# Seven half-size products in place of eight: Strassen's algorithm in the second MLP product

## The chip, the core and the metric

The kernel runs on one core of one Trainium2 chip. The metric is the device time of one execution in microseconds (us), the median over runs. The engines named below are TensorE (PE; its weight loads are PEld), VectorE (DVE), ScalarE (ACT), GpSimd (POOL) and SyncE (SP, which here issues loads, transposes and some stores). Each runs its own instructions in program order; they meet at semaphores.

## The reference, cut to what matters

```python
# attention: q, k, v are (8, 8, 576, 64); phi gives 128 features per position
q_p = phi(q, cos_w, sin_w); k_p = phi(k, cos_w, sin_w)      # relu(x)*cos, relu(x)*sin
kv = einsum('bhsf,bhsd->bhfd', k_p, v); z = sum(k_p, axis=2)
attn = einsum('bhsf,bhfd->bhsd', q_p, kv) / (einsum('bhsf,bhf->bhs', q_p, z) + 1e-06)
x = attn.transpose(0, 2, 1, 3).reshape(8, 576, 512)
# mixer: U (576, 32), V (32, 576), w_ch1 (512, 2048), w_ch2 (2048, 512)
u = x + (x.transpose(0, 2, 1) @ U @ V).transpose(0, 2, 1)
out = u + maximum(u @ w_ch1, 0) @ w_ch2
```

Inputs and output are fp32. The first MLP product is `u @ w_ch1`, the second is `hid @ w_ch2` with `hid` the relu of the first. The kernel multiplies in bf16 and sums in fp32.

## The kernel before

A batch has 576 rows: four chunks of 128 and a tail of 64. Two batches make a pair, and their two tails make one more chunk of 128 rows.

The attention of a batch goes through `q_prep` and `k_prep` (relu times cos or sin, ten instructions of 128x512 each for q and for k, on DVE or ACT), `v_prep` (casts of v to bf16, mostly on POOL), transposes of q by DMA (`qtr_dma`), `kv_unit`, `x_unit` (matmuls into the PSUM tile `x_ps`, which has one buffer, then reciprocal and scaling on DVE), `A_unit` (x times U), and `u_unit` (V times that into `va_ps`, then DVE adds x and writes `u_bf`). `utr_dma` transposes `u_bf` into `uT`.

The MLP of a batch: `g1_main(b, j)` makes 128 of the 2048 hidden columns for four chunks of rows, with four matmuls of 512 columns into `g_ps`; ACT takes the relu into `hid`. `g1_tail` does the same for a pair's tail chunk with matmuls of 128 columns, into `hid_tl`. `g2_part(pr, cc, part)` does a quarter of the second product for one chunk of rows: four matmuls of 512 columns, of the 16 that sum into a bank of `o_ps`. After the fourth quarter DVE adds `u_bf` and writes `o_sb`, which is stored.

The order is written by hand. `slots` is a list of such units: for each pair, 16 of `g1_main` for the even batch, 16 for the odd, four of `g1_tail`, 36 of `g2_part` (in the first pair the even batch's second product stands behind its first). One slot is four matmuls of 512 columns. `todo` names what is issued behind each slot: the attention of later batches, by `PLAN` and `attention_plan`. A `PLAN` entry has the slot of `kv_unit`, the place of the preparations against it, the engines for q and k, the place of the q transposes, and the places of the next batch's loads. `spare(at)` picks the PSUM tag for a unit issued behind slot `at`. PSUM has the tags `g` (three banks), `o` (two), `X` (two banks as one tile) and `T` (one).

## Time and profile before

| | us |
|---|---|
| median of three runs (lowest, highest) | 312.73 (312.23, 314.8) |
| span of the profiled execution, first to last instruction | 314.4 |
| PE busy | 305.0 |
| DVE busy | 154.3 |
| ACT busy | 136.3 |
| POOL busy | 53.0 |
| first product, `g1_main` matmuls busy (512) | 117.6 |
| second product, `g2_part` matmuls on `hid` and `hid_tl` busy (592) | 134.8 |

The profile gives no other time of its execution than the span; it lies at the upper end of the three runs. Busy times of PE contain the overlap of one matmul with the next, so a rate is read from the start of one to the start of the next. In the groups of the profile a line holds: code line, engine, operation, tiles written and read, shapes, count, busy time, mean ns of one, and the idle time ahead with what ended it. In a timeline a line holds start, length (of several merged: from the first start to the last end), engine, code line, operation, tiles.

### The profile page before, as it was taken

The numbers are of one execution on the slowest core, as the hardware profiler recorded it, in microseconds if no ns is written. First come the engines' busy times: TensorE is split into PE (matmuls) and PEld (weight loads), VectorE is DVE, ScalarE is ACT, GpSimd is POOL, SyncE is SP. The second block draws the span as 40 slices with busy tenths as digits, with TensorE's granted clock in tenths as the row PEclk, the third lists the DMA queues.
The fourth block names the chain that finished last, engine by engine and source line by source line (L and its number), as shares of the span: only waits on it lengthen the run. The fifth ranks groups of instructions, "written<-read, shape, count | busy, mean of one in ns | idle before, by whom it ended". The sixth has DMA issues, their size and how long they took to land.

```text
span 314.4 us, 5674 instructions
## 1 busy us (share of the span) xinstructions
PE 305.0 (97%) x2305; PEld 159.2 (51%) x2305; DVE 154.3 (49%) x341; ACT 136.3 (43%) x229; POOL 53.0 (17%) x96
## 2 busy tenths in 40 slices
PE   5989999999999899999999999999999999999995
PEld 2665555445745344474455444574455444474443
DVE  4787845696778567036525585036526530002111
ACT  2835660265560256659500266659500266640000
POOL 8410400240041106102321310002321100000000
PEclk9789999999999999999999999999999999999999
DMA  7999799969997979993699769942791140001131
GB/s 211 353 248 253 175 186 263 292 154 238 300 131 170 250 197 206 217 294 108 158 204 318 242 101 170 301 118 52 167 167 69 67 86 0 0 2 67 67 100 69
DMA packets 86027, 53.21 MB, mean 169 GB/s; under 512 B 54258, under 2 KB 83218, under 8 KB 86002
## 3 DMA queue, kind: packets, MB, share of 16 engines
q1 hardware_dynamic: 79298, 41.36, 56.9%
q0 software_dynamic: 6560, 11.43, 14.5%
q8 instruction: 18, 0.29, 0.4%
q14 instruction: 7, 0.06, 0.1%
q10 hardware_dynamic: 144, 0.07, 0.1%
HBM read 36.86 MB, written 9.44 MB: 147 GB/s over the span
## 4 chain that ended last, share of the span: by engine, by line
PE 84%; DMA 7%; DVE 5%; ACT 2%; issue 1%; DVEq 0%; ACTq 0%
PE o_ps L587 36%; PE g_ps L534 32%; PE gt_ps L554 5%; PE kv_ps L294 3%; DMA vst<-in_v_dram 3%; PE x_ps L401 2%; DMA q_tlT<-q_tl 2%; PE va_ps L446 2%; DMA uT<-u_bf 2%; DVE q_p L260 2%; DVE k_p L260 1%; ACT k_p L258 1%; PE t_ps L311 1%; PE a_ps L426 1%; ACT v_ext L108 1%
## 5 line engine op out<-in xcount | busy, mean ns | idle before, releaser
L543 ACT ACTIVATE hid<-g_ps 128x512 bf16<-128x512 f32 x128 | 76.3, 598 | 106.2 <-PE g_ps L534 106.1
L587 PE MATMUL o_ps<-w_bf,hid 128*128 128x512 bf16 (+2 forms) x528 | 120.0, 372 | 0.0
L534 PE MATMUL g_ps<-uT,w_bf 128*128 128x512 bf16 x512 | 117.6, 379 | 1.0 <-DMA uT<-u_bf 1.0
L534 PEld LDWEIGHTS <-w_bf 128*128 128x128 bf16 x512 | 48.9, 98 | 59.2 <-issue 2.0
L587 PEld LDWEIGHTS <-hid 128*128 128x128 bf16 x528 | 48.3, 98 | 50.7 <-issue 0.8
L597 DVE TENSOR_TENSOR o_sb<-u_bf,o_ps 128x512 f32<-128x512 bf16 (+2 forms) x33 | 22.1, 669 | 56.3 <-PE o_ps L587 56.2
L608 POOL DMA_DIRECT2D out_dram<-o_sb x24 | 15.2, 633 | 128.3 <-DVE o_sb L597 67.2
L453 DVE TENSOR_TENSOR u_bf<-x_bf,va_ps 128x512 bf16<-128x512 bf16 x32 | 21.8, 685 | 10.0 <-PE va_ps L446 9.9
L110 POOL CAST v_ext<-vst 128x512 bf16<-128x512 f32 (+1 forms) x28 | 20.0, 739 | 38.1 <-DMA vst<-in_v_dram 35.6
L110 DVE CAST kv<-kv_ps 128x260 bf16<-128x260 f32 x15 | 6.4, 429 | 38.0 <-PE kv_ps L294 38.0
L411 DVE TENSOR_TENSOR x_bf<-x_ps,rec 128x512 bf16<-128x512 f32 x28 | 19.4, 691 | 1.0
L358 DVE TENSOR_SCALAR rec<-x_ps 128x8 f32<-128x8 f32 (+1 forms) x35 | 5.8, 165 | 23.9 <-PE x_ps L401 23.4
L554 PE MATMUL gt_ps<-uT_tl,w_bf 128*128 128x128 bf16 x256 | 15.9, 219 | 0.0
L554 PEld LDWEIGHTS <-w_bf 128*128 128x128 bf16 x256 | 14.7, 98 | 0.9
L260 DVE TENSOR_SCALAR q_p<-qst,cosw 128x512 bf16<-128x512 f32 x24 | 13.7, 581 | 3.0 <-DMA qst<-in_q_dram 3.0
L587 PE MATMUL o_ps<-w_bf,hid_tl 128*128 128x512 bf16 x64 | 14.8, 379 | 0.0
L401 PEld LDWEIGHTS <-q_pT 128*128 128x128 bf16 x224 | 10.7, 98 | 6.6 <-DVE x_bf L411 0.6
L294 PEld LDWEIGHTS <-k_p 128*128 128x128 bf16 x256 | 11.2, 97 | 4.3 <-ACT v_tl L108 1.1
L258 ACT ACTIVATE k_p<-kst,sinw 128x512 bf16<-128x512 f32 x19 | 13.3, 712 | 0.0
L294 PE MATMUL kv_ps<-v_ext,k_p 128*128 128x65 bf16 x256 | 11.8, 193 | 1.0 <-ACT v_tl L108 0.8
L561 ACT ACTIVATE hid_tl<-gt_ps 128x512 bf16<-128x512 f32 x16 | 9.6, 598 | 6.6 <-PE gt_ps L554 6.6
L446 PE MATMUL va_ps<-A_sb,V_bf 128*128 128x512 bf16 x32 | 12.1, 379 | 0.1
(125 smaller groups left out, 235.5 us busy)
## 6 DMA issues: line engine op xcount, KB each, us to landing
qst<-in_q_dram SPq DMA_DIRECT2D x14, 512.0 KB, 6.1
kst<-in_k_dram SPq DMA_DIRECT2D x14, 512.0 KB, 8.5
vst<-in_v_dram SPq DMA_DIRECT2D x12, 512.0 KB, 8.4
out_dram<-o_sb POOLq DMA_DIRECT2D x24, 256.0 KB, 3.1
w_bf<-in_moe_w_ch_dram POOLq DMA_DIRECT2D x8, 512.0 KB, 10.6
out_dram<-o_sb SPq DMA_DIRECT2D x7, 256.0 KB, 2.4
qst<-in_q_dram SPq DMA_DIRECT2D x2, 640.0 KB, 6.5
kst<-in_k_dram SPq DMA_DIRECT2D x2, 640.0 KB, 11.1
```

Of the source, the lines that this page charges most:

```text
L110: eng.tensor_copy(out=o, in_=i)
L260: eng.tensor_scalar(out=o, in0=i, scalar1=0.0, scalar2=w, op0=ALU.max, op1=ALU.mult)
L294: nc.tensor.matmul(out=acc[:, i, :], lhsT=k_p[b][:, c, h, :] if c < 4 else k_tl[:, h, :], rhs=v_tl[:, h, :] if c == 4 and b < 2 else vx[:, ...
L401: nc.tensor.matmul(out=acc[:, g, i * E : i * E + E], lhsT=qT_of(b, c, h), rhs=kv_sb[b][:, h, :], start=True, stop=True,)
L411: nc.vector.tensor_tensor(out=x_of(b, c, rows).rearrange("p (g i d) -> p g i d", g=2, d=D), in0=view[:, :, :, 0:D], in1=rec[rows].unsqueez ...
L446: nc.tensor.matmul(out=va, lhsT=V_bf[:, c, :], rhs=A_of(b), start=True, stop=True)
L453: nc.vector.tensor_tensor(out=u_bf[b][:, c, :] if c < 4 else u_tl[b // 2], in0=x_of(b, c), in1=va, op=ALU.add,)
L534: nc.tensor.matmul(out=g_ps.rearrange("p (c t) -> p c t", c=4), lhsT=w1_bf[:, d, j * P : j * P + P], rhs=uT[b][:, :, d, :], start=(d == 0) ...
L543: nc.scalar.activation(out=hid[b][:, j, :], in_=g_ps, func=AF.Relu, bias=0.0, scale=1.0)
L554: nc.tensor.matmul(out=g_ps[:, jj, :], lhsT=w1_bf[:, d, j * P : j * P + P], rhs=uT_tl[pr][:, d, :], start=(d == 0), stop=(d == 3),)
L587: nc.tensor.matmul(out=o[:, cols], lhsT=lhs[:, j, c * P : c * P + P], rhs=w2_bf[:, j, cols], start=(j == 0), stop=(j == NJ - 1),)
L597: nc.vector.tensor_tensor(out=o_sb[:, cols], in0=u[:, cols], in1=o[:, cols], op=ALU.add)
```

## The change

Batch 0 and the tail chunks keep the plain product. For batches 1 to 7, the 512 rows of `hid` and the 512 columns of w2 are halved, and the 2048 hidden indices are split into even and odd blocks of 128. Seven products of half size, `w_part(b, n)` with n from 0 to 13 (two slots to a step), are summed in two banks of PSUM, `oA` and `oB`. Each step has 16 matmuls of 256 columns. Steps 0 and 2, and 4 and 6, go to bank A; steps 1, 3 and 5 to bank B; a bank that is opened again, or summed further, has been read out before. The sums and differences of blocks that the products need are made on DVE: `w2_form` once (T1 to T4), `hid_form` per batch in halves (S1, S2, S4, and the third in place in `hid`). After step 0 ACT casts bank A to `w_sum`; after step 1 DVE adds bank B to it and POOL makes three additions of `w_sum` and `u_bf` into `o_sb`; DVE adds the banks after steps 2 to 6.

The second product of each batch now stands right behind its first (for the odd batch, behind the tail units). A pair has 70 slots (the first) or 68. `PLAN` is moved to match. Several tiles have fewer buffers, and two chunks leave in one store.

```diff
-    zero = const.tile([P, 512], BF16)
+    zero = pool.tile([P, 512], BF16, tag="o_sb", bufs=2, name="zero")
...
-    A_sb = [const.tile([P, DM], BF16, name=f"A_sb{i}") for i in range(4)]
+    A_sb = [const.tile([P, DM], BF16, name=f"A_sb{i}") for i in range(3)]
...
+    def O2():
+        turn[0] += 1
+        return (OB, OA)[turn[0] % 2]
...
-            u_bf[b] = pool.tile([P, 4, DM], BF16, tag="u_bf", bufs=3, name="u_bf")
+            u_bf[b] = pool.tile([P, 4, DM], BF16, tag="u_bf", bufs=2, name="u_bf")
...
-            hid[b] = pool.tile([P, NJ, 512], BF16, tag="hid", bufs=2, name="hid")
+            hid[b] = pool.tile([P, NJ, 512], BF16, tag="hid", bufs=1, name="hid")
...
+    def store(eng, b, c, o):
+        nines_o = out[b].rearrange("(m k) n -> m (k n)", k=9)
+        eng.dma_start(
+            out=bass.AP(
+                tensor=nines_o.tensor, offset=nines_o.offset + c * DM,
+                ap=[[9 * DM, TS], [5 * DM, 2], [1, 2 * DM]],
+            ),
+            in_=o.rearrange("p c n -> p (c n)"),
+        )
...
+    def w2_form(n, half):
+        r = slice(half * 4, half * 4 + 4)
+        a, b_, op = (
+            (w2_block(0, 1, r), w2_block(0, 0, r), ALU.subtract),
+            (w2_block(1, 1, r), T[0][:, r, :], ALU.subtract),
+            (w2_block(1, 1, r), w2_block(0, 1, r), ALU.subtract),
+            (w2_block(1, 0, r), T[1][:, r, :], ALU.subtract),
+        )[n]
+        V_.tensor_tensor(out=T[n][:, r, :], in0=a, in1=b_, op=op)
...
+    def hid_block(b, i, r, rows=slice(0, KB)):
+        h = hid[b].rearrange("p (k i) t -> p k i t", i=2)
+        return h[:, rows, i, r * 256 : r * 256 + 256]
+
+    def hid_form(b, n, half):
...
+        if n == 1:
+            a, b_, op = hid_block(b, 0, 1, r), hid_block(b, 1, 1, r), ALU.add
+        elif n == 2:
+            a, b_, op = s_forms[b, 1][:, r, :], hid_block(b, 0, 0, r), ALU.subtract
+        elif n == 3:
+            a, b_, op = hid_block(b, 0, 0, r), hid_block(b, 0, 1, r), ALU.subtract
+        else:
+            a, b_, op = hid_block(b, 1, 0, r), s_forms[b, 2][:, r, :], ALU.subtract
+        V_.tensor_tensor(out=o, in0=a, in1=b_, op=op)
...
+    def w_part(b, n):
+        step, half = divmod(n, 2)
...
+        bank = w_ps[b, step % 2]
+        lhs, rhs = (
+            (lambda: hid_block(b, 0, 0), w2_block(0, 0)),
+            (lambda: s_forms[b, 2], T[1]),
+            (lambda: hid_block(b, 1, 0), w2_block(1, 0)),
+            (lambda: s_forms[b, 1], T[0]),
+            (lambda: s_forms[b, 3], T[2]),
+            (lambda: s_forms[b, 4], w2_block(1, 1)),
+            (lambda: hid_block(b, 1, 1), T[3]),
+        )[step]
+        lhs = lhs()
+        opens = step in (0, 1, 3, 4)
+        for k_ in range(half * 4, half * 4 + 4):
+            for g in range(2):
+                nc.tensor.matmul(
+                    out=bank[:, g, :], lhsT=lhs[:, k_, g * P : g * P + P], rhs=rhs[:, k_, :],
...
+        if n < 2:
+            for f in ((1, 2), (4, 3))[n]:
+                hid_form(b, f, 1)
...
+        if step == 0:
+            w_sum[b] = pool.tile([P, 2, HD], FP32, tag="w_sum", bufs=1, name="w_sum")
+            cast(A_, w_sum[b], bank)
+        elif step == 1:
...
+            add(V_, w, w, bank)
+            add(G_, o1[:, :, hi], w, u[:, 2:4, hi])
+            add(G_, o0[:, :, hi], w, u[:, 0:2, hi])
+            add(G_, o1[:, :, lo], w, u[:, 2:4, lo])
+        elif step == 2:
+            o0 = o_sb[b, 0]
+            add(V_, o0[:, :, lo], u[:, 0:2, lo], bank)
+        elif step == 3 or step == 4:
+            o = o_sb[b, 1][:, :, hi]
+            add(V_, o, o, bank)
...
+    def first_units(b):
+        starts[b] = len(slots)
+        lay([lambda j=j: g1_main(b, j) for j in range(NJ)], False)
+        if b > 0:
+            for i in range(4):
+                beside.setdefault(starts[b] + 9 + i, []).append(
+                    lambda i=i: hid_form(b, (1, 2, 4, 3)[i], 0)
+                )
+
+    def second_units(b):
+        lay([lambda n=n: w_part(b, n) for n in range(14)], True)
...
     PLAN = {
-        2: (46, -15, V_, V_, -10, (-5, -4, -4)),
-        3: (60, -11, V_, A_, -6, (7, 7, 22)),
+        2: (45, -15, V_, V_, -10, (-5, -4, -4)),
+        3: (64, -11, V_, A_, -6, (7, 7, 12)),
         4: (100, -20, V_, V_, -12, (-6, -6, -6)),
-        5: (130, -20, A_, A_, -13, (-7, -7, -7)),
-        6: (172, -20, V_, V_, -12, (-6, -6, -6)),
+        5: (134, -20, A_, A_, -13, (-7, -7, -7)),
+        6: (168, -20, V_, V_, -12, (-6, -6, -6)),
         7: (202, -20, A_, A_, -13, ()),
     }
...
+    for n in range(4):
+        for half in range(2):
+            todo.setdefault(33 + 2 * n + half, []).append(
+                lambda n=n, half=half: w2_form(n, half)
+            )
```

More of the change, by code (lines that the diff above doesn't have):

```diff
@@ L230, in spread_v @@
         cast(eng, V_tl, v_ps[:, 1, 0:TS])
+    G3, T1, OA, OB = ("g", 3), ("T", 1), ("oA", 1), ("oB", 1)
+    turn = [0]
+    def O2():
+        turn[0] += 1
+        return (OB, OA)[turn[0] % 2]
     k_p, q_p, q_pT, kv_sb, x_bf = {}, {}, {}, {}, {}
@@ L418, in A_of @@
     def A_of(b):
-        return A_sb[b % 4]
+        return A_sb[b % 3]
     def A_unit(b, tag, bufs, eng=None, n0=0, n1=DM, a_ps=None):
@@ L440, in u_unit @@
         if b not in u_bf:
-            u_bf[b] = pool.tile([P, 4, DM], BF16, tag="u_bf", bufs=3, name="u_bf")
+            u_bf[b] = pool.tile([P, 4, DM], BF16, tag="u_bf", bufs=2, name="u_bf")
         if c == 4:
-            u_tl[b // 2] = pool.tile([P, DM], BF16, tag="u_tl", bufs=2, name="u_tl")
+            u_tl[b // 2] = pool.tile([P, DM], BF16, tag="u_tl", bufs=1, name="u_tl")
         va = ps.tile([P, DM], FP32, tag=tag, bufs=bufs, name="va_ps")
@@ L463, in uTt_alloc @@
         if pr not in uT_tl:
-            uT_tl[pr] = pool.tile([P, 4, P], BF16, tag="uT_tl", bufs=2, name="uT_tl")
+            uT_tl[pr] = pool.tile([P, 4, P], BF16, tag="uT_tl", bufs=1, name="uT_tl")
     def utr_dma(b, c0, c1):
@@ L564, in g1_tail, with o_alloc, store_eng, g2_part @@
         )
-    o_ps = {}
-    def g2_part(pr, cc, part):
-        last = pr == NPAIR - 1 and cc == 8
-        if part == 0 or last and part == 3:
-            tag, bufs = ("g", 3) if pr == 0 and 2 <= cc < 4 else ("o", 2)
-            o_ps[pr, cc] = ps.tile([P, DM], FP32, tag=tag, bufs=bufs, name="o_ps")
-        o = o_ps[pr, cc]
-        if cc == 4:
-            b, lhs, c, u = None, hid_tl[pr], 0, u_tl[pr]
-        else:
-            b, c = (2 * pr, cc) if cc < 4 else (2 * pr + 1, cc - 5)
-            lhs, u = hid[b], u_bf[b][:, c, :]
+    def store(eng, b, c, o):
[7 more added lines that the diff above has]
+        )
+    o_sb = {}
+    def o_alloc(b, r):
+        if (b, r) not in o_sb:
+            o_sb[b, r] = pool.tile([P, 2, DM], FP32, tag="o_sb", bufs=2, name="o_sb")
+        return o_sb[b, r]
+    def store_eng(b):
+        return nc.gpsimd if b < B - 2 else nc.sync
+    o_ps = {}
+    def g2_part(cc, part):
+        if part == 0:
+            tag, bufs = G3 if cc >= 2 else O2()
+            o_ps[cc] = ps.tile([P, DM], FP32, tag=tag, bufs=bufs, name="o_ps")
+        o = o_ps[cc]
+        for j in range(part * 4, part * 4 + 4):
+            nc.tensor.matmul(
+                out=o, lhsT=hid[0][:, j, cc * P : cc * P + P], rhs=w2_bf[:, j, :],
+                start=(j == 0), stop=(j == NJ - 1),
+            )
+        if part < 3:
+            return
+        r, g = divmod(cc, 2)
+        o_s = o_alloc(0, r)
+        nc.vector.tensor_tensor(out=o_s[:, g, :], in0=u_bf[0][:, cc, :], in1=o, op=ALU.add)
+        if g == 1:
+            store(store_eng(0), 0, 2 * r, o_s)
+    def g2_tail(pr, part):
+        last = pr == NPAIR - 1
+        if part == 0 or last and part == 3:
+            tag, bufs = OB if part == 0 else OA
+            o_ps[pr] = ps.tile([P, DM], FP32, tag=tag, bufs=bufs, name="ot_ps")
+        o = o_ps[pr]
         if last:
@@ L587, in g2_part @@
             nc.tensor.matmul(
-                out=o[:, cols],
-                lhsT=lhs[:, j, c * P : c * P + P],
-                rhs=w2_bf[:, j, cols],
-                start=(j == 0),
-                stop=(j == NJ - 1),
+                out=o[:, cols], lhsT=hid_tl[pr][:, j, :], rhs=w2_bf[:, j, cols],
+                start=(j == 0), stop=(j == NJ - 1),
             )
@@ L595, in g2_part @@
             return
-        o_sb = pool.tile([P, DM], FP32, tag="o_sb", bufs=4, name="o_sb")
+        if part == 2 or not last:
+            o_alloc(B + pr, 0)
+        o_s = o_sb[B + pr, 0][:, 0, :]
         nc.vector.tensor_tensor(
-            out=o_sb[:, cols], in0=u[:, cols], in1=o[:, cols], op=ALU.add
+            out=o_s[:, cols], in0=u_tl[pr][:, cols], in1=o[:, cols], op=ALU.add
         )
-        eng = nc.gpsimd if pr < NPAIR - 1 else nc.scalar if part == 3 and last else nc.sync
-        if cc == 4:
-            for i in range(2):
-                eng.dma_start(
-                    out=out[2 * pr + i].rearrange("(m k) n -> m k n", k=9)[:, 4, :],
-                    in_=o_sb[i * TS : i * TS + TS, :],
-                )
-        else:
-            eng.dma_start(
-                out=out[b].rearrange("(m k) n -> m k n", k=9)[:, c : c + 6 : 5, cols],
-                in_=o_sb[:, cols],
-            )
+        for i in range(2):
+            eng = store_eng(2 * pr) if part == 2 or not last else (nc.sync, nc.scalar)[i]
+            eng.dma_start(
+                out=out[2 * pr + i].rearrange("(m k) n -> m k n", k=9)[:, 4, cols],
+                in_=o_s[i * TS : i * TS + TS, cols],
+            )
@@ new lines, with w2_block @@
+    HD = DM // 2
+    KB = NJ // 2
+    w2_h = w2_bf.rearrange("p (k i) n -> p k i n", i=2)
+    T = [const.tile([P, KB, HD], BF16, name=f"T{i}") for i in range(1, 5)]
+    def w2_block(i, h, r=slice(0, KB)):
+        return w2_h[:, r, i, h * HD : h * HD + HD]
+    def w2_form(n, half):
[7 more added lines that the diff above has]
+        V_.tensor_tensor(out=T[n][:, r, :], in0=a, in1=b_, op=op)
@@ new lines @@
+    s_forms = {}
+    def hid_block(b, i, r, rows=slice(0, KB)):
+        h = hid[b].rearrange("p (k i) t -> p k i t", i=2)
+        return h[:, rows, i, r * 256 : r * 256 + 256]
+    def hid_form(b, n, half):
+        if (b, n) not in s_forms:
+            s_forms[b, n] = (
+                hid_block(b, 0, 1) if n == 3 else
+                pool.tile([P, KB, 256], BF16, tag=f"S{n}", bufs=1, name=f"S{n}")
+            )
+        r = slice(half * 4, half * 4 + 4)
+        o = s_forms[b, n][:, r, :]
+        if n == 1:
[7 more added lines that the diff above has]
+        V_.tensor_tensor(out=o, in0=a, in1=b_, op=op)
@@ new lines, with add @@
+    w_ps, w_sum = {}, {}
+    def w_part(b, n):
+        step, half = divmod(n, 2)
+        if n == 0:
+            w_ps[b, 0] = ps.tile([P, 2, HD], FP32, tag="oA", bufs=1, name="wa_ps")
+        if n == 2:
+            w_ps[b, 1] = ps.tile([P, 2, HD], FP32, tag="oB", bufs=1, name="wb_ps")
+        bank = w_ps[b, step % 2]
[12 more added lines that the diff above has]
+            for g in range(2):
+                nc.tensor.matmul(
+                    out=bank[:, g, :], lhsT=lhs[:, k_, g * P : g * P + P], rhs=rhs[:, k_, :],
+                    start=(opens and k_ == 0 and g == 0),
+                    stop=(k_ == KB - 1 and g == 1), skip_group_check=not opens,
+                )
+        if n < 2:
+            for f in ((1, 2), (4, 3))[n]:
+                hid_form(b, f, 1)
+        if half == 0:
+            return
+        u = u_bf[b]
+        lo, hi = slice(0, HD), slice(HD, DM)
+        def add(eng, o, x, y):
+            eng.tensor_tensor(out=o, in0=x, in1=y, op=ALU.add)
+        if step == 0:
+            w_sum[b] = pool.tile([P, 2, HD], FP32, tag="w_sum", bufs=1, name="w_sum")
+            cast(A_, w_sum[b], bank)
+        elif step == 1:
+            w = w_sum[b]
+            o0, o1 = o_alloc(b, 0), o_alloc(b, 1)
+            add(V_, w, w, bank)
[8 more added lines that the diff above has]
+            add(V_, o, o, bank)
+        elif step == 5:
+            o = o_sb[b, 0][:, :, hi]
+            add(V_, o, o, bank)
+            store(store_eng(b), b, 0, o_sb[b, 0])
+        else:
+            o = o_sb[b, 1][:, :, lo]
+            add(V_, o, o, bank)
+            store(store_eng(b), b, 2, o_sb[b, 1])
@@ L624, with lay, lay_all @@
     ORD = (4, 0, 1, 2, 3)
+    slots, second, starts = [], [], {}
+    def lay(units, in_second):
+        slots.extend(units)
+        second.extend([in_second] * len(units))
+    def first_units(b):
[5 more added lines that the diff above has]
+                    lambda i=i: hid_form(b, (1, 2, 4, 3)[i], 0)
+                )
+    def second_units(b):
+        lay([lambda n=n: w_part(b, n) for n in range(14)], True)
+    beside = {}
+    def lay_all():
+        for pr in range(NPAIR):
+            e, o = 2 * pr, 2 * pr + 1
+            first_units(e)
+            if pr == 0:
+                lay([lambda cc=cc, p=p: g2_part(cc, p) for p in range(4) for cc in range(4)], True)
+            else:
+                second_units(e)
+            first_units(o)
+            lay([lambda j=j, pr=pr: g1_tail(pr, j) for j in range(4)], False)
+            second_units(o)
+            lay([lambda p=p, pr=pr: g2_tail(pr, p) for p in range(4)], True)
+    lay_all()
     def spare(at):
-        if at < 72:
-            return ("o", 2) if 32 <= at < 52 else ("g", 3)
-        return ("o", 2) if at % 72 < 36 else ("g", 3)
+        if second[at]:
+            return T1 if not all(second[at : at + 2]) else G3
+        return T1 if any(second[at : at + 3]) else O2()
     QORD = (4, 0, 1, 2, 3)
     PLAN = {
-        2: (46, -15, V_, V_, -10, (-5, -4, -4)),
-        3: (60, -11, V_, A_, -6, (7, 7, 22)),
+        2: (45, -15, V_, V_, -10, (-5, -4, -4)),
+        3: (64, -11, V_, A_, -6, (7, 7, 12)),
         4: (100, -20, V_, V_, -12, (-6, -6, -6)),
-        5: (130, -20, A_, A_, -13, (-7, -7, -7)),
-        6: (172, -20, V_, V_, -12, (-6, -6, -6)),
+        5: (134, -20, A_, A_, -13, (-7, -7, -7)),
+        6: (168, -20, V_, V_, -12, (-6, -6, -6)),
         7: (202, -20, A_, A_, -13, ()),
@@ L682 @@
     TL = (0, 1, 2, 3, 4)
-    O2, G3 = ("o", 2), ("g", 3)
     def den_mm(b, h0, h1, d_ps):
@@ L715, in xh_norm @@
         )
-    T1 = ("T", 1)
     def warm(n, tag=G3):
@@ L753, in first_chain @@
         kv_unit(b, 0, *T1)
-        kv_unit(b, 1, *O2, A_)
+        kv_unit(b, 1, *O2(), A_)
         d0 = ps.tile([P, 2, 512], FP32, tag="X", bufs=1, name="d_ps")
@@ L760, in first_chain @@
         den_mm(b, 4, 8, d[1])
-        x0 = [xh_mm(b, c, 0, *t) for c, t in zip(ORD, (G3, G3, G3, O2, O2))]
+        x0 = [xh_mm(b, c, 0, *t) for c, t in zip(ORD, (G3, G3, G3, O2(), O2()))]
         recip(rec[0], d[0])
@@ L769, in first_chain @@
         spread_v(A_)
-        x1 += [xh_mm(b, c, 4, *t) for c, t in zip(ORD[2:], (G3, G3, O2))]
+        x1 += [xh_mm(b, c, 4, *t) for c, t in zip(ORD[2:], (G3, G3, O2()))]
         for n in range(5):
@@ L775, in first_chain @@
         t = [u03[:, i, :].rearrange("p (c t) -> p c t", c=4) for i in range(2)]
-        a_ps = ps.tile([P, DM], FP32, tag="o", bufs=2, name="a_ps")
+        ao = O2()
+        a_ps = ps.tile([P, DM], FP32, tag=ao[0], bufs=ao[1], name="a_ps")
         a_mm(b, a_ps, 0, 256, range(5))
         cast(A_, A_of(b)[:, 0:256], a_ps[:, 0:256])
-        for tag, bufs in (T1, O2):
+        for tag, bufs in (T1, O2()):
             t.insert(-1, ps.tile([P, 4, P], FP32, tag=tag, bufs=bufs, name="uT_ps"))
@@ L798 @@
     for c in TL:
-        tg = G3 if c < 3 else O2
+        tg = G3 if c < 3 else O2()
         t_q.append(ps.tile([P, H, P], BF16, tag=tg[0], bufs=tg[1], name="t_ps"))
@@ L832 @@
     q_prep(1, 0, (V_, V_))
-    beside = {}
     def at(j, *thunks):
@@ L845 @@
             at(n - 2, lambda c=c: q_prep(1, c, (V_, V_)))
-        tg = ("T", 1) if n % 2 else O2
+        tg = T1 if n % 2 else O2()
         at(1 + n, lambda c=c, tg=tg: qtr_unit(1, c, eng=V_, tag=tg[0], bufs=tg[1]))
@@ L851 @@
     for c in range(4):
-        at(5 + c, lambda c=c: u_unit(0, c, *O2))
+        at(5 + c, lambda c=c: u_unit(0, c, *O2()))
     for hg in range(2):
@@ L872 @@
     for n, c in enumerate(ORD):
-        at((32, 42, 43, 44, 45)[n], lambda c=c: u_unit(1, c, *O2))
+        at((32, 42, 43, 44, 45)[n], lambda c=c: u_unit(1, c, *O2()))
     at(33, lambda: utr_dma(1, 4, 5))
-    slots, todo = [], {}
-    for pr in range(NPAIR):
-        e, o = 2 * pr, 2 * pr + 1
-        slots += [
-            lambda j=j, e=e: g1_main(e, j) for j in range(NJ)
-        ]
-        early = [(cc, p) for p in range(4) for cc in range(4)] if pr == 0 else []
-        slots += [lambda cc=cc, p=p: g2_part(0, cc, p) for cc, p in early]
-        slots += [lambda j=j, o=o: g1_main(o, j) for j in range(NJ)]
-        slots += [lambda j=j, pr=pr: g1_tail(pr, j) for j in range(4)]
-        slots += [
-            lambda cc=cc, p=p, pr=pr: g2_part(pr, cc, p)
-            for cc in range(9) for p in range(4) if (cc, p) not in early
-        ]
+    todo = {}
     for j, ts_ in beside.items():
         todo[j] = list(ts_)
+    for n in range(4):
+        for half in range(2):
+            todo.setdefault(33 + 2 * n + half, []).append(
+                lambda n=n, half=half: w2_form(n, half)
+            )
     def put(at, thunk):
```

## The prediction

> **What bounds the kernel now.** I read the page's busy shares first, then the chain of waits at its undisturbed end, then the groups by shape, then the order of time of DVE, POOL, PE and ACT where the change puts its new work.

> ```profile
> PE 305.0 (97%) x2305; PEld 159.2 (51%) x2305; DVE 154.3 (49%) x341; ACT 136.3 (43%) x229; POOL 53.0 (17%) x96
> ```
> TensorE sets the time. Its rates stand in the chain of waits (start, us, what):
> ```profile
> 254.61 21.58 PE g_ps L534 x100
> 276.19 3.57 PE gt_ps L554 x64
> 279.77 31.14 PE o_ps L587 x160
> ```
> 100 matmuls of 512 columns in 21.58 us are 215.8 ns each; 64 of 128 columns in 3.57 us are 55.8 ns each. That is 0.417 ns per column and 2.5 ns fixed, and each has a weight load of its own. So only fewer columns, or a wait, move the end.

> Two groups give sizes for VectorE (DVE) and one for ScalarE (ACT):
> ```profile
> L110 DVE COPY q_pT<-t_ps 128x1024 bf16<-128x1024 bf16 x6 | 4.0, 684 | 1.7 <-PE t_ps L323 1.1 <-PE t_ps L311 0.6
> L708 DVE TENSOR_TENSOR x_bf<-xh_ps,rec 128x256 bf16<-128x256 f32 x8 | 2.7, 401 | 0.0
> L543 ACT ACTIVATE hid<-g_ps 128x512 bf16<-128x512 f32 x128 | 76.3, 598 | 106.2 <-PE g_ps L534 106.1
> ```
> DVE is half idle over the span, but not everywhere. The stretches (PE, PEld, DVE, ACT, POOL busy):
> ```profile
> 60.00:80.00 20.00, 19.94 (x154) 10.52 (x153) 16.72 (x33) 11.26 (x20) 4.57 (x8) 1.00 0.83 213
> 80.00:100.00 20.00, 19.71 (x202) 11.05 (x200) 16.07 (x40) 9.15 (x15) 4.16 (x7) 1.00 1.10 211
> 260.00:280.00 20.00, 20.00 (x142) 11.02 (x140) 0.00 (x0) 13.77 (x24) 0.00 (x0) 1.00 0.00 1
> ```
> From 60 to 100 us DVE is over 80% busy: there it prepares batches 2 and 3. In order of time:
> ```profile
> 63.64 2.76 DVE L260 TENSOR_SCALAR q_p<-qst,cosw 128x512 bf16<-128x512 f32 x1
> 66.31 0.47 DVE L260 TENSOR_SCALAR q_p<-qst,sinw 128x512 bf16<-128x512 f32 x1
> 66.70 0.47 DVE L260 TENSOR_SCALAR q_p<-qst,cosw 128x512 bf16<-128x512 f32 x1
> ...
> 72.64 0.47 DVE L260 TENSOR_SCALAR k_p<-kst,sinw 128x512 bf16<-128x512 f32 x1
> 73.04 1.87 DVE L453 TENSOR_TENSOR u_bf<-x_bf,va_ps 128x512 bf16<-128x512 bf16 x3
> ```
> ```profile
> 63.26 2.85 POOL L110 CAST v_ext<-vst 64x512 bf16<-64x512 f32 x5
> ```
> ```profile
> 72.46 0.38 PE L446 MATMUL va_ps<-A_sb,V_bf 128*128 128x512 bf16 x1
> 72.68 1.03 PE L534 MATMUL g_ps<-uT,w_bf 128*128 128x512 bf16 x4
> 73.76 0.38 PE L446 MATMUL va_ps<-A_sb,V_bf 128*128 128x512 bf16 x1
> ```
> Three things to see. DVE preparations follow each other every 0.396 us, u_bf additions every 0.60. While POOL ran five casts in a row, one DVE preparation that lasts 0.47 took 2.76. And the matmul at 73.76 came 0.22 us late (72.68 + 0.863 = 73.54): its bank came free only with the u_bf addition of 73.04. DVE already stood at PE's heels there. ACT's preparations follow each other every 0.62 us:
> ```profile
> 143.28 0.71 ACT L258 ACTIVATE q_p<-qst,sinw 128x512 bf16<-128x512 f32 x1
> 143.89 0.70 ACT L258 ACTIVATE q_p<-qst,cosw 128x512 bf16<-128x512 f32 x1
> ```

> **The change, part by part.** *Saved on PE.* A second product is 64 matmuls of 512 columns, 64 x 0.2158 = 13.81 us. It becomes 7 steps of 16 matmuls of 256 columns; the trace has none, and 55.8 and 215.8 ns bound it; on the straight line 2.5 + 256 x 0.417 = 109.1 ns. 112 x 0.1091 = 12.22 us, a step 1.75. Saved 1.59, over seven batches **11.1 us**. [...]

> *Added on DVE.* Once eight forms of w2 (T), per batch eight forms of hid (S), and six additions from PSUM in place of four. A form is 128x1024 bf16 with both operands in SBUF; no row has one. Nearest: the copy of 128x1024 bf16, 684 ns, so every 0.60 us; that I take. Below: 0.40, as the preparations. Above: one element at a time, from 401 ns (256) and 685 (512) to 1.27, every 1.18. Per batch ACT gets one cast (0.6) and POOL three additions of 128x512; POOL's one-operand cast is 0.57 to 0.62; two operands may take twice that.

> *Where this meets PE.* With t = 0 at a batch's first Strassen matmul, PE needs S2 whole at 2.6, ACT's cast of bank A at 3.5, DVE's w_sum addition (frees bank B) at 5.2, the next addition at 7.0, and so on every 1.75. All engines run in program order, so I add up what stands ahead of each in the changed order.

> (1) First product of batch 1. All eight T forms and two S forms stand ahead of the u_bf addition that ran at 73.04: 10 x 0.60. The third va_ps matmul waits for it: **+6.0** (4.0 to 11.8). Nothing covers it, since DVE was already 0.2 late.

> (2) Second product of batch 1. Each step has, on DVE, an x_unit of batch 2 (1.04), two preparations (0.8) and an addition (0.6), 2.44 us against PE's 1.75 + 0.26 for the x_ps matmuls. x_ps has one buffer, so PE waits for it: about 0.4 a step after a first 1.0, together 1.8; 0.3 of such waits were there before, so +1.5. POOL's three additions start first and shut the preparations out as its casts did: 3 x 0.57 less the addition beside it, +0.7 (0 to 2.3 at twice the price). **+2.2.** [...]

> (3) Transposes of u(2). SP issues the last q_pT(3) transpose ahead of them, and its q_p(3) is now ready only 2 to 3 us before u(2), not 9 (89.6 against 99.1). A q_pT issue takes 1.8 to 5.2 us. PE waited 0.98 us at 105.48 before; **+1.0** (0 to 3.7).

> (4) Batches 2 and 4 start their second product right behind the first, while DVE prepares batches 4 and 6. Over the last six units of the first product DVE gets four forms, five u additions and ten preparations, 2.4 + 3.0 + 4.0 = 9.4 us, in 6.5 us of PE, 0.3 of them waiting for PE; 3.2 are left at t = 0. For batch 2: two forms later S2 is ready at 4.4, not 2.6 (wait 1.75). Then six preparations, two forms and the w_sum addition, 4.3: at 8.65 against 7.0 (1.65). Then four preparations and an addition, 2.25 against 1.75 (0.45). Together 3.9. For batch 4 the order differs: one va_ps waits 1.9 for its bank, then 1.8 and 0.45: 4.2. **+8.1** (5 to 17, the ends by the forms). DVE starts first here, so POOL waits and the preparations don't.

> (5) Batches 3 and 5. Between the second last relu of the first product and the w_sum cast, ACT's queue has 12 preparations of batch 5 or 7 (7.4), five relus (2.9) and the cast (0.6). They start 0.76 after that product unit and end at 11.8; PE, through the tail units and two steps, wants the cast at 9.2. The cast frees bank A for step 2. **2.6 each, +5.2** (4 to 5.4).

> (6) Batches 6 and 7 have no preparations beside them: 0. One hid buffer: the next relu waits for a PE step that lies ahead of it on PE anyway, 0. One u_tl, two u_bf, the shared o_sb: their readers end a first product (14 us) earlier, 0; without that cover each would cost one store, 3.1 us to landing. Half as many stores on POOL, 0.63 us of issue each, off the path. Two last stores in place of one: +0.2.

> **Sum:** -11.1 + 6.0 + 2.2 + 1.0 + 8.1 + 5.2 + 0.2 = +11.6. The profiled span is 314.4, 1.7 over the median of 312.73 (runs 312.23 to 314.8), so the profile after should span some 326 and the median be 312.73 + 11.6 = **324.3 us**.

> **Rivals.** *A, not slower: the queues are empty at t = 0.* If DVE and ACT have worked off their preparations before the first Strassen matmul of batches 2 to 5 (decided by a rest under about 0.4 us, what the last relu's 0.76 and two forms leave of S2's 2.6 in a free batch), (4) and (5) fall away: -1.7, **311.0**. For it: both are under half busy overall, and DVE did nothing from 260 to 280. Against: the order puts the preparations right there, in engines that can't pass over them.

> *B, faster: (1) is covered as well,* if batch 2's preparations begin some 6 us earlier: **305.0**. Against: they wait behind the additions of batch 0, which follow PE's matmuls by 0.2 us.

> *C, much slower: a form handles one element at a time,* 1.18 for 0.60. (1) gains 5.8, batches 2 and 4 4.6 each, the other five about 1.5 each: 22.5 more, **347**. For it: every DVE addition in the trace runs so. Against: those read fp32 from PSUM; the bf16 copy of 1024 elements took no longer than a 512 one.

> **How the numbers follow.** Forecast (slower, 316 to 334) 0.58; A 0.12; B 0.22, more than its mechanism deserves, for covers that I don't see; C 0.08. About 1% is what a measurement of this kernel can tell from no change: faster 0.22, same 0.11, slower 0.67 (a little of A lies above 1%). The forecast's own range is 316 to 334. The full one reaches down to B: 304 to 334; C and the rest outside are under 2 in 10.

> **What would show it.** Right: wa_ps and wb_ps matmuls 109 ns apart; a PE gap of about 6 us near 73 to 80 us, released by DVE u_bf; gaps in the second products of batches 2 and 4 released by DVE (S2, w_sum), of 3 and 5 by ACT's w_sum; none in 6 and 7, which should each be 1.6 us shorter. PE busy near 90%, DVE near 64%. Wrong: no such gaps, or forms nearer 0.4 or 1.2 us than 0.65.

## The result, and the profile after

The changed kernel takes 341.3 us (median of four runs, 341.0 to 342.1) where the kernel before takes 312.5 (312.2 to 314.8): a ratio of 1.0881, interval 1.0827 to 1.0934. The forecast was slower, 324.3 us; the time is 17 us above it and 7 above the top of the range. The profiled execution spans 338.8 us, 24.4 more than that of before.

From the page after, the busy shares, and the clock that TensorE was granted, in tenths of its full speed, in 40 slices of the span:
```profile
PE 304.1 (90%) x2641; PEld 194.1 (57%) x2641; DVE 205.7 (61%) x419; ACT 139.5 (41%) x236; POOL 71.6 (21%) x105
...
PEclk9799999995999989899999989999999999999998
```
The shares are near those forecast (PE 90%, DVE 64%). The second row is not: a slice is 8.5 us, and the clock is at half in the tenth and dips in the 15th, 17th and 24th, in the middle of a kernel that in the profile of before held full clock from 26 us to its last matmul.

The chain of waits at its end (start, us, what) has the products by themselves:
```profile
301.54 13.81 PE g_ps L541 x64
...
318.93 1.75 PE wa_ps L708 x16
320.67 1.75 PE wb_ps L708 x16
```
A step of 16 matmuls of 256 columns takes 1.75 us, 109 ns each, as on the straight line. A second product takes 12.2 us in place of 13.8. The saving is there.

Groups by shape (out<-in, count | busy us, mean ns of one | idle time before them):
```profile
L722 POOL TENSOR_TENSOR o_sb<-w_sum,u_bf 128x512 f32<-128x512 f32 x21 | 26.8, 1297 | 114.2 <-DVE w_sum L722 102.8 <-DVE rec L365 11.4
L684 DVE TENSOR_TENSOR S<-hid 128x1024 bf16<-128x1024 bf16 x14 | 9.5, 682 | 10.9 <-ACT hid L550 10.9
```
A form takes 0.68 us, as the copy did. A POOL addition takes 1.30 on average, not 0.57; half of the additions took 1.15 or less.

What TensorE waited for (in all us, how often, longest):
```profile
PE va_ps L453 <- DVE u_bf L460: 7.8, 2, 5.9
PE g_ps L541 <- DMA uT<-u_bf: 4.4, 1, 4.4
PE wa_ps L708 <- ACT w_sum L108: 3.8, 2, 2.1
PE wb_ps L708 <- DVE S L684: 2.1, 1, 2.1
...
PE x_ps L408 <- DVE x_tl L418: 2.0, 1, 2.0
PE x_ps L408 <- DVE x_bf L418: 2.0, 4, 1.2
PE wb_ps L708 <- DVE w_sum L722: 1.7, 1, 1.7
```
Nearly every stall of the prediction stands here under the name it gave. The first one, in order of time on DVE and on PE:
```profile
78.32 0.69 DVE L684 TENSOR_TENSOR S<-S,hid 128x1024 bf16<-128x1024 bf16 x1
78.93 0.68 DVE L460 TENSOR_TENSOR u_bf<-x_bf,va_ps 128x512 bf16<-128x512 bf16 x1
```
```profile
72.72 1.03 PE L541 MATMUL g_ps<-uT,w_bf 128*128 128x512 bf16 x4
79.66 0.58 PE L453 MATMUL va_ps<-A_sb,V_bf 128*128 128x512 bf16 x1 [5.92 <-DVE u_bf L460]
80.04 1.91 PE L541 MATMUL g_ps<-uT,w_bf 128*128 128x512 bf16 x4
81.75 0.63 PE L453 MATMUL va_ps<-A_sb,V_bf 128*128 128x512 bf16 x1
```
The addition that ran at 73.04 before runs at 78.93, behind the forms: 5.9 us. But look at what follows. Four matmuls that start at 80.04 give way to the next at 81.75, after 1.71 us; they take 0.86 elsewhere. The stretches (PE, PEld, DVE, ACT, POOL busy, granted clock):
```profile
77.00:80.00 3.00, 0.34 (x1) 0.10 (x1) 2.97 (x6) 0.00 (x0) 0.00 (x0) 0.55 0.93 259
80.00:84.00 4.00, 4.00 (x28) 2.09 (x27) 3.12 (x6) 0.60 (x1) 0.00 (x0) 0.50 1.09 319
84.00:88.00 4.00, 4.00 (x65) 3.16 (x64) 0.43 (x1) 1.79 (x3) 0.61 (x1) 0.98 0.72 219
```
During the gap the granted clock fell to half, and it stayed there for 4.4 us after work had come back. In shorter windows the same is seen from 118.3 to 121.7, 142.2 to 145.6 and 200.2 to 203.6 us: 3.4 us each, always behind a gap, and beginning 0.8 to 1.3 us after the gap has ended.

**The ledger**, from 61.5 us on, where both kernels start batch 1's first product: saved columns -11.1; waits of the profile 23.7 more than before; half clock, each window's busy time times the clock that it lacks, 7.4. A wait is counted from the end of a matmul's row, which lies 0.16 us behind the start of the next in a full stream (0.38 against 0.216), so eleven new waits hide 1.8 more at their restarts. That is 21.8 of 24.4; of the rest, 2.6, the end has 0.7 (4.2 us behind the last matmul, 3.5 before); what is left is waits under 0.25 us, not placed one by one.

### The profile page after: what moved, and what is told of

The parts are those of the page before. It is cut to its first block, busy times and chain, and to the rows that moved or that the text cites. A ratio compares the mean times of both kernels' runs of the same rounds, so it can differ in the third digit from the quotient of the medians.

```text
span 338.8 us, 6435 instructions
## 1 busy us (share of the span) xinstructions
PE 304.1 (90%) x2641; PEld 194.1 (57%) x2641; DVE 205.7 (61%) x419; ACT 139.5 (41%) x236; POOL 71.6 (21%) x105
## 5 line engine op out<-in xcount | busy, mean ns | idle before, releaser
L541 PE MATMUL g_ps<-uT,w_bf 128*128 128x512 bf16 x512 | 125.6, 389 | 4.4 <-DMA uT<-u_bf 4.4
L708 PEld LDWEIGHTS <-hid 128*128 128x128 bf16 x448 | 44.2, 99 | 14.4 <-issue 7.9
L722 POOL TENSOR_TENSOR o_sb<-w_sum,u_bf 128x512 f32<-128x512 f32 x21 | 26.8, 1297 | 114.2 <-DVE w_sum L722 102.8
L708 PEld LDWEIGHTS <-S 128*128 128x128 bf16 x336 | 32.8, 98 | 8.5 <-DVE S L684 2.4
L708 PE MATMUL wa_ps<-w_bf,hid 128*128 128x256 bf16 x224 | 28.7, 283 | 3.9 <-ACT w_sum L108 3.8
L110 POOL CAST v_ext<-vst 128x512 bf16<-128x512 f32 (+1 forms) x28 | 19.8, 733 | 55.7 <-DMA vst<-in_v_dram 55.7
L708 PE MATMUL wb_ps<-T,S 128*128 128x256 bf16 x224 | 27.0, 273 | 3.8 <-DVE S L684 2.1
L708 PE MATMUL wa_ps<-T,hid 128*128 128x256 bf16 x224 | 26.9, 273 | 0.4 <-DVE o_sb L722 0.3
L453 PE MATMUL va_ps<-A_sb,V_bf 128*128 128x512 bf16 x32 | 12.6, 393 | 8.8 <-DVE u_bf L460 7.8
L110 DVE CAST kv<-kv_ps 128x260 bf16<-128x260 f32 x15 | 6.4, 428 | 18.4 <-PE kv_ps L301 18.4
L575 POOL DMA_DIRECT2D out_dram<-o_sb x12 | 7.6, 631 | 47.2 <-DVE o_sb L609 24.9
L722 DVE TENSOR_TENSOR o_sb<-o_sb,wb_ps 128x512 f32<-128x512 f32 x14 | 9.6, 686 | 12.1 <-PE wb_ps L708 11.2
L722 DVE TENSOR_TENSOR o_sb<-o_sb,wa_ps 128x512 f32<-128x512 f32 x14 | 9.6, 685 | 12.1 <-PE wa_ps L708 12.1
L684 DVE TENSOR_TENSOR S<-hid 128x1024 bf16<-128x1024 bf16 x14 | 9.5, 682 | 10.9 <-ACT hid L550 10.9
```

The costliest lines, as they stand in the source:

```text
L110: eng.tensor_copy(out=o, in_=i)
L453: nc.tensor.matmul(out=va, lhsT=V_bf[:, c, :], rhs=A_of(b), start=True, stop=True)
L541: nc.tensor.matmul(out=g_ps.rearrange("p (c t) -> p c t", c=4), lhsT=w1_bf[:, d, j * P : j * P + P], rhs=uT[b][:, :, d, :], start=(d == 0) ...
L575: eng.dma_start(out=bass.AP(tensor=nines_o.tensor, offset=nines_o.offset + c * DM, ap=[[9 * DM, TS], [5 * DM, 2], [1, 2 * DM]],), in_=o.re ...
L684: V_.tensor_tensor(out=o, in0=a, in1=b_, op=op)
L708: nc.tensor.matmul(out=bank[:, g, :], lhsT=lhs[:, k_, g * P : g * P + P], rhs=rhs[:, k_, :], start=(opens and k_ == 0 and g == 0), stop=(k ...
```

## The experiments

Two theories run through the expectations. **W**: the extra time is the waits that the changed order makes. **W+C**: the waits, and the half clock that follows long ones. Ratios are against the kernel before on the same chip, whose median was between 312.5 and 314.8 us; they are to be set beside 1.0881. One per cent is 3.1 us.

From one profiled execution to the next, 0 (e8_three_earlier), 3.4 (the changed kernel) or 6.8 us (before) of half clock fall into the first 60 us. So the profiles are also compared without these, from the first matmul of batch 1's first product to the end of the span:

| | us | | us |
|---|---|---|---|
| before | 253.0 | changed | 277.4 |
| e1_T_early | 273.6 | e7_two_earlier | 249.0 |
| e2_plain | 257.7 | e8_three_earlier | 249.3 |
| e3_fill | 274.8 | e9_u_first | 249.4 |
| e4_mixed | 265.4 | e10_plain_shared | 256.8 |
| e5_all | 254.5 | e11_q3 | 273.0 |
| e6_before_forms | 258.8 | e12_tail_buf | 273.8 |

**e1_T_early, the T forms moved.**
```
-            todo.setdefault(33 + 2 * n + half, []).append(
+            todo.setdefault(17 + 4 * n + 2 * half, []).append(
```

> Only the eight T forms move, from slots 33 to 40 to every second slot from 17 to 31, where DVE is half idle. Theory W+C (waits as the queues make them, and a TensorE clock that falls to half after a long gap): the 5.9 us gap in batch 1's first product shrinks to about 1.2 (two S forms stay ahead), and the half clock from 77 to 84 us goes with it, 4.4 us of PE work at half speed, 2.2 lost: 341.3 - 4.7 - 2.2 = 334.4. Rival W (waits alone, the clock costs nothing in the end): 336.6. Rival D (DVE's backlog is only passed on to the next wait): 339 or more.

1.0789 (1.0728 to 1.0851): 0.9% won, 2.9 us, of 6.9 expected; the interval overlaps that of the changed kernel, so the time alone shows little. The first gap shrank from 5.9 to 3.0 and 0.6, not to 1.2. Two T forms still ran at 62.6 and 65.1 us, when DVE was already behind, and beside POOL's casts a preparation took 3.5 us (2.8 in the kernel before):
```profile
65.74 3.52 DVE L267 TENSOR_SCALAR q_p<-qst,cosw 128x512 bf16<-128x512 f32 x1
```
```profile
66.14 2.84 POOL L110 CAST v_ext<-vst 64x512 bf16<-64x512 f32 x5
```
The half clock stayed too (79 to 83 us), now 3.4 us long, and a wait of 1.3 us came new at 52 us: x_ps waits for DVE, which stood 2.0 us until the load of w2 had landed that the T form at 50.19 reads. Rival D had a part of it: a backlog is passed on where the engine has no room either.

**e2_plain, the changed order with plain second products.** In w_part, 64 matmuls of 512 columns over the 14 slots and four additions:
```
+        for m in range(64 * n // 14, 64 * (n + 1) // 14):
+            cc, j = divmod(m, NJ)
...
+            nc.tensor.matmul(
+                out=o, lhsT=hid[b][:, j, cc * P : cc * P + P], rhs=w2_bf[:, j, :],
```

> The changed order of products, tiles and DMA calls stays, but the second products of batches 1 to 7 are the plain ones (64 matmuls of 512 columns spread over the same 14 slots, four DVE additions, no T or S forms, no w_sum, no POOL additions). Theory W+C: the gaps of batch 1's first product and those that wait for S, w_sum or DVE u_bf go, the wait for the transposes of u(2) and for the shared o_sb of the pair's tail may stay: 313 to 319. Rival O (the order itself costs the time, the algorithm only its part): 325 or more. Rival N (the order costs nothing): 312.5.

1.0186 (1.0136 to 1.0236), 318.3 on the scale of before, within W+C. No clock is lost after 12 us. The order, its smaller buffers and its two single banks cost 5.8 us themselves (4.7 by the table); PE waits 0.78 us at each pair's tail for DVE's last addition. The rest of the loss came with what this version leaves out: forms, copies and additions of the algorithm.

**e3_fill, idle matmuls in two gaps.**
```
+    todo[44].insert(0, lambda: fill(22, "X", 1))
+    todo.setdefault(69, []).append(lambda: fill(16, "g", 3))
```

> The changed kernel with idle matmuls put into two of its gaps, ahead of the instruction that waits: 22 of 512 columns (4.7 us) in the 5.9 us gap of batch 1's first product, 16 (3.5 us) in the 4.4 us gap ahead of batch 2's first product. No wait is shorter. Theory W+C: the granted clock stays at 1.00 from 77 to 84.5 and from 118.2 to 121.4 us, 2.2 + 1.6 us are won: 337.5. Rival W: the waits end when they ended, 341.3, or the matmuls come in the way, 342 to 345.

1.0681 (1.0589 to 1.0774), 2.0% below the changed kernel; in the profiled spans 336.0 against 338.8. The ratio is that of two executions, with mean granted clocks of 0.999 and 0.993. The other two, at 0.988 and 0.983, spanned 338.0 and 337.9 us, still less than the changed kernel's 338.8 to 340.2 at 0.967 to 0.972. W is out: PE did 8.2 us more work and the time fell. The same stretches as above, now:
```profile
77.00:80.00 3.00, 1.82 (x10) 0.71 (x9) 2.96 (x6) 0.00 (x0) 0.00 (x0) 1.00 0.96 251
80.00:84.00 4.00, 3.17 (x32) 1.59 (x31) 2.72 (x5) 1.17 (x2) 0.00 (x0) 1.00 1.12 314
```
The clock was full in every slice of this execution, also behind gaps that were not filled. Only the first two half clocks are gone by the filling; for the others the last section has the reason. Yet the span gained less than the 7.4 us of the ledger, since waits came back that a slow TensorE had covered: in batch 2's second product w_sum and o_sb are waited for 1.4 and 1.2 us, 0 and 0 in the changed kernel. All waits of 0.25 us or more outside the two filled gaps grew by 4.3 us, and 7.4 - 4.3 is near the 2.8 gained. Half clock and a late DVE are partly the same time.

**e4_mixed, preparations shared.** For batches 4 to 7:
```
+            qe = (V_, A_) if b > 3 else (q_eng, q_eng)
+            ke = (V_, A_) if b > 3 else (k_eng, k_eng)
```

> Only the engines of the preparations of batches 4 to 7 change: of each pair one on DVE and one on ACT, in place of both on DVE (batches 4 and 6) or both on ACT (5 and 7). Theory W+C: DVE is 2 us less behind at the start of the second products of batches 2 and 4, ACT 3.7 us less in 3 and 5, so the waits for S2, u_bf, w_sum (2.1 + 2.1 + 3.8 + 1.7 us) shrink to under 2 together, and the half clock after 142 us goes (1.7): 331. Rival A (ACT is then late with the w_sum cast of batches 2 and 4 in its turn): 335 to 338. Rival D (other waits come in their place): 339 or more.

1.0429 (1.0346 to 1.0513): 4.5% won, 14 us, more than expected. The waits for S2, u_bf and w_sum in batches 2 to 5, 9.8 us together, are gone but for 0.3 for u_bf and 0.4 in each of three batches for o_sb; the x_ps wait of batch 4 stays (2.4), and the clock holds behind 121 us. Items (4) and (5) of the prediction are shown to come from what stands in the queues of DVE and ACT, and rival A is out. That no half clock followed the 2.4 us wait goes with its place, cut into 1.86 and 0.49 us (last section).

**e6_before_forms, one stall by itself in the kernel before.** Ten subtractions of blocks of w2, of a form's size, into a scratch tile `scr`:
```
+    for n in range(8):
+        put(33 + n, lambda n=n: form(4 * (n % 2)))
+    for n in range(2):
+        put(41 + n, lambda n=n: form(4 * n))
```

> The kernel before with ten additions of 128x1024 bf16 on DVE into a scratch tile in slots 33 to 42, where the changed kernel has eight T and two S forms; their results are used by nothing. It prices this stall by itself. Theory W+C: the third va_ps waits 5.5 to 6.2 us, and TensorE then runs one or two periods of 3.4 us at half clock, part of them in the gap: 1.7 to 2.2 lost; before + 8 (ratio 1.026). Rival W: the wait alone, before + 6.0 (1.019). Rival B (covered after all): before + 0 to 2.

1.0257 (1.0182 to 1.0332), 8.0 us, W+C's figure; by time alone W's 1.019 is inside the interval too, but the trace has the clock:
```profile
79.53 0.59 PE L446 MATMUL va_ps<-A_sb,V_bf 128*128 128x512 bf16 x1 [5.60 <-DVE u_bf L453]
79.90 1.91 PE L534 MATMUL g_ps<-uT,w_bf 128*128 128x512 bf16 x4
```
The stretch behind it, its granted clock third from the end:
```profile
80.00:83.50 3.50, 3.50 (x10) 1.27 (x9) 1.95 (x4) 0.60 (x1) 0.00 (x0) 0.50 0.96 302
```
Ten forms in the wrong hour cost 5.6 us of wait, and the four matmuls behind it, from 79.90 to 81.61, take 1.71 us again: 2.0 us lost at half clock. Batch 1's first product, up to its tail, takes 23.4 us in place of 15.9, 7.5 more: wait and clock, not the wait alone. Then 1.7 come back, 0.98 of it the wait for the transposes of u(2), which is gone. The net 5.8 us (table) happens to be W's figure; that the medians gave W+C's 8 is partly luck.

**e11_q3 and e12_tail_buf, two terms one by one.** One execution each, beside 313.4 us for the kernel before, so the times are weak; what was moved is read from the traces.
```
-                put(f_at + 2 * n, q_prep, c, (q_eng, q_eng))
+                put(f_at + n, q_prep, c, (q_eng, q_eng))
...
-        3: (64, -11, V_, A_, -6, (7, 7, 12)),
+        3: (64, -13, V_, A_, -8, (7, 7, 12)),
```

> The changed kernel with one thing moved: batch 3's q preparations two slots earlier and in consecutive slots, its three q transposes two slots earlier on SP. Theory W+C: SP is free when u(2) is ready; the 4.4 us wait ahead of batch 2's first product shrinks by the 2.4 us that q_pT's issue held the transposes up, to about 2. Rival L (the landing of the transposes beside the stores sets it): 3.5 to 4.4.

335.1 us. Both expectations missed: the 4.4 us wait is gone altogether. SP's queue in the changed kernel, then here:
```profile
102.48 5.76 SPq L344 DMA_TRANSPOSE q_pT<-q_p  x2
108.34 5.62 SPq L476 DMA_TRANSPOSE uT<-u_bf  x2
```
```profile
95.55 6.04 SPq L344 DMA_TRANSPOSE q_pT<-q_p  x2
105.82 3.80 SPq L476 DMA_TRANSPOSE uT<-u_bf  x2
```
With q_pT 7 us earlier, u(2)'s transposes are issued as soon as u is ready, and they also land in 4.5 and 4.6 us in place of 8.3 and 5.8. The hold-up by q_pT was the smaller part: in the changed kernel the first half of u was ready at 107.0 and its transpose issued at 108.3, 1.3 us later. The x_ps wait of batch 1 grew to 2.1 us meanwhile, with a half clock behind it.
```
-            o_alloc(B + pr, 0)
-        o_s = o_sb[B + pr, 0][:, 0, :]
+            o_sb[B + pr, 0] = pool.tile([P, DM], FP32, tag="o_tl", bufs=1, name="o_tl")
+        o_s = o_sb[B + pr, 0]
```

> The changed kernel with one thing moved: the output rows of each pair's tail get a buffer of their own and no longer wait for one of the two o_sb buffers. Theory W+C: the tail's addition, which came 3.2 us after its last matmul at 193.6 us, follows it at once, so the 2.0 us gap of x_ps at 198.9 goes, and with it the half clock from 200 to 204 us: 3.7 us shorter in that stretch. Rival V (the load of v for batch 5 is what is waited for): the gap stays.

335.6 us; the 2.0 us gap and the half clock behind it are gone, and by the table the kernel is 3.6 us shorter, 3.7 expected. The addition of the tail's output on DVE, in the changed kernel and here:
```profile
196.89 0.69 DVE L634 TENSOR_TENSOR o_sb<-u_tl,ot_ps 128x512 f32<-128x512 bf16 x1 [3.25 <-PE g_ps L541]
```
```profile
193.16 0.69 DVE L634 TENSOR_TENSOR o_tl<-u_tl,ot_ps 128x512 f32<-128x512 bf16 x1 [0.43 <-PE ot_ps L625]
```
The first names a matmul as its releaser that had nothing to do with it. It waited for a store: POOL issued it at 188.72 us, and it landed 8.05 us later, at 196.77.

**e5_all, e7_two_earlier, e8_three_earlier, e9_u_first: the causes moved together.** In e5_all the T forms go to slots 16 to 27, the preparations of batches 2 to 7 are shared, but for k of batches 2 and 3, which stays on DVE (batch 2's k is shared from e8_three_earlier on); batch 3's q work comes earlier and the tail has its own buffer. Then batch 2's chain comes two and three slots earlier (last lines), and the second halves of the odd batches' S forms go beside the tail units, in e9_u_first behind u.
```
-            todo.setdefault(33 + 2 * n + half, []).append(
+            todo.setdefault(((16, 17, 19, 21), (23, 25, 26, 27))[half][n], []).append(
...
+            qe = (V_, A_)
...
+            for i in range(4):
+                beside.setdefault(len(slots) + i, []).append(
+                    lambda i=i, o=o: hid_form(o, (1, 2, 4, 3)[i], 1)
+                )
...
-        2: (45, -15, V_, V_, -10, (-5, -4, -4)),
-        3: (64, -11, V_, A_, -6, (7, 7, 12)),
+        2: (42, -15, V_, V_, -10, (-5, -4, -4)),
+        3: (64, -15, V_, A_, -10, (7, 7, 12)),
```

> The changed kernel with its seven half-size products kept, and each stall's cause moved: T forms spread over slots 16 to 27; the preparations of all of batches 2 to 7 shared between DVE and ACT one each; batch 3's q preparations in slots 51 to 55 and its transposes two slots earlier, so that SP is free for u(2); a buffer of its own for the output rows of each pair's tail. Theory W+C: all gaps over 1 us go, no half clock after 30 us, the columns saved show: before - 11.1 + 1 to 3, that is 303 where before takes 312.5 (ratio 0.97). Rival A (ACT is late in its turn in the first product of batch 1): 308 to 318. Rival S (seven half-size products gain nothing here even without waits, since additions and forms cost PE in other ways): 312 or more.

1.0126 (1.0060 to 1.0193), so W+C's 303 was missed. By time it lies in the ranges of A and S, but the trace has no wait for ACT in batch 1's first product, and with waits left it doesn't test S; e10_plain_shared does. The gap of 5.9 is gone, but 2.7 us ahead of batch 2's first product stayed, with a half clock behind, and 2.0 for x_ps. Here SP was free (u ready at 97.87, issue at 97.89), yet the second transpose landed 7.7 us after its issue; why that was 4.6 in e11_q3 is not settled.

> The version with all causes moved, and two of the rest too: batch 2's whole chain (kv, x, A, u, transposes) two slots earlier, batch 3's q preparations and transposes as well; and the second halves of the S forms of batches 1, 3, 5 and 7 beside the tail units ahead of the second product, where DVE is idle, in place of inside its first two steps. Theory W+C: the 2.7 us wait for the transposes of u(2) falls to about 1 and the half clock after it (1.7) goes, the 2.0 us x_ps wait in batch 1's second product falls under 1: 4.4 less than the version before it, ratio 0.999 (0.99 to 1.005). Rival D (DVE can't have batch 2's k preparations ready two slots earlier, kv waits instead): 1.01 or more.

0.9923 (0.9883 to 0.9963), inside the range: no wait for the transposes (about 1 expected), 1.1 for x_ps (under 1 expected).

> The same with batch 2's chain three slots earlier and its k preparations shared between DVE and ACT too. Theory W+C: no wait for the transposes of u(2), ratio 0.995 (0.985 to 1.003). Rival A (ACT's queue, with ten preparations more beside sixteen relus of batch 1, runs late and g_ps waits for its banks): 1.005 or more.

0.9877 (0.9825 to 0.9930), inside the range: a version faster than both kernels, by the medians 3.8 us below before. Half clock at the start has a part in this: all its four executions had a mean clock of 0.997 or more, and only three of the twelve of before. Against those three (312.1, 312.6 and 312.8) it gains 1.6. From batch 1's first product on (table) e7_two_earlier, e8_three_earlier and e9_u_first are alike, 3.6 to 4.0 us below before, so the step from two slots to three shows no gain. Its page:
```profile
PE 293.5 (95%) x2641; PEld 190.0 (61%) x2641; DVE 201.5 (65%) x404; ACT 146.8 (47%) x251; POOL 70.6 (23%) x105
...
PEclk9999999999999999999999999999999999999999
```
TensorE is busy 10.6 us less than in the changed kernel, at full clock throughout; the longest wait after the first 10 us is 1.0.

> The version with batch 2's chain three slots earlier, with one order changed: beside the tail units, DVE adds u first and then makes the second halves of the S forms. There the version before shows three waits of 1.0 us for DVE u_bf (at 154.7, 189.5, 225.7 us), of which two stand beside the tail units of batches 3 and 5 and follow the S forms in DVE's queue. Theory W+C: those two go, 2 to 2.4 us with their restarts, ratio 0.980 (0.974 to 0.988). Rival S2 (the forms are then late for the second step): 0.988 or more.

0.9952 (0.9915 to 0.9990), outside the range, with the same span as e8_three_earlier, 309.4. It is in S2's range, but no step waits for S in the trace. The three waits shrank only from 1.0 to 0.9, so the order of S and u was not their cause. Beside a tail unit DVE has 0.6 for u, 0.4 for a preparation and 0.6 for a form, 1.6 us, while PE takes 0.89 + 0.22: too much work, in any order.

**e10_plain_shared, the schedule of e8_three_earlier with the plain products of e2_plain.**

> That version (preparations shared between DVE and ACT, batch 2's chain three slots earlier, the tail's own buffer) with the plain second products in place of the seven half-size ones: no T or S forms, no w_sum, no POOL additions. It tells what the algorithm itself is worth where its work is covered, and what the other edits are worth alone. Theory W+C: no waits over 1 us but those for DVE's o_sb at the pair tails; before + 0 to 2, ratio 1.00 to 1.007, so that the seven products are worth 5 to 8 us of their 11.1. Rival E (the sharing and the earlier chain made the gain, the algorithm nothing): 0.985 to 0.992, as the version with it.

1.0230 (1.0189 to 1.0271), above W+C's range. Rival E is out: the sharing alone gives nothing (e2_plain had 1.0186). Against e8_three_earlier the seven products are worth 3.5%, 11 us, by the medians and 9.7 in the spans. But 2.1 of these lie ahead of batch 1's first product, where this execution had 3.4 us of half clock and that of e8_three_earlier none. By the table it is 7.5 of the 11.1, within W+C's 5 to 8, once the additions stand where DVE and ACT have room.

## Why the prediction was wrong

The sum was +11.6 us; the medians differ by 28.8. Point by point:

- **Saved on PE, -11.1:** right, 109 ns a matmul.
- **(1) +6.0:** 5.9.
- **(2) +2.2:** 2.6 (1.25, 0.42 and 0.97), though POOL's additions were priced at less than half (0.57 us, where 1.30 was measured). It was right partly by luck.
- **(3) +1.0 (0 to 3.7):** 3.4 more than before. Mechanism right, size off: a short hold-up was taken, and the transposes' longer issue (3.2 and 2.3 us; 1.2 and 1.6 in e11_q3) and landing were left out. Moving q_pT away ended both in e11_q3, though by e5_all it is not the only thing that sets the landing.
- **(4) +8.1:** 5.9, being 2.1 in batch 2 and 1.9, 1.7 and 0.3 in batch 4. In batch 2 the waits for w_sum and o_sb did not come, since TensorE was at half clock; e3_fill shows both, and e11_q3, without half clock there, 1.4 for w_sum. That POOL waits where DVE started first was measured: in the trace of before a cast of some 0.6 us took 4.03 at 120.57 us, beside preparations on DVE that went on every 0.396, and in the changed kernel an addition of 1.15 took 2.51 at 145.43.
- **(5) +5.2:** 3.8 (2.1 and 1.7).
- **(6) 0:** 2.0 us in batch 4. The shared o_sb was named, with the wrong cover: its reader does not end a first product earlier at a pair's tail, and the store took 8.05 us to land, not 3.1.

The waits summed to 22.5 in the prediction and come to 23.7 in the profile, with misses both ways, so that they agree so well is partly luck. Rival C's slow forms, A's empty queues and B's cover are out, and batches 6 and 7 ran without a gap as said. **The step that failed is the sum itself: it costed a stall at its own length.** Behind four of the stalls TensorE ran at half speed, from 80 to 84 us for one, at a granted clock of 0.50. The half clock, 7.4 us, is in no term; nor are 1.8 us at restarts and 2.4 in small waits and at the end (the ledger's 2.6 less the 0.2 that were forecast). It was there to be read: in the trace of before TensorE waits 2.4 us at 8 us, and runs at half clock for 3.4 us behind it, from 8.06 to 11.47 (the granted clock is third from the end):
```profile
8.23 1.03 PE L323 MATMUL t_ps<-ident,q_p 128*128 128x128 bf16 x8 [2.37 <-ACT q_p L258]
```
```profile
8.50:11.00 2.50, 2.50 (x21) 1.95 (x19) 2.12 (x5) 1.93 (x4) 0.87 (x2) 0.50 1.07 356
```

The last 4.2 us are the measure's: the sum carried a difference of spans to the median of before. The profiled execution of before is not a typical one: two stretches of half clock lie in its first 26 us. In the later runs of before the time is 1.7 to 1.8 us above the span, so the median of 312.5 stands for a span of some 310.7, 3.7 below the profiled 314.4; after's 338.8 is 0.7 below its own median's. Of these 4.4 us, 0.2 fall away because the sum started from 312.73. In all, 1.2 of waits, 7.4 of clock, 1.8 of restarts, 2.4 of small waits and the end, and 4.2 of the measure make the 17.0 us.
